# A second layer in seven products on four token-tile pairs, with the low halves on GpSimd

## The chip, the cores and the metric

The kernel runs on one core of one Trainium2 chip. The time is device microseconds of that core, from one launch that does everything; the figure of a kernel is the median of its runs. The profile is one execution, recorded by the hardware profiler.

## The reference

Three stages follow each other: an attention with fixed masks, a mixture of experts whose weights P come from a Sinkhorn balancing, and a second mixture that routes each token to two experts. The change lies in the middle stage:

```python
def _moe_ref(x, w_gate, w1, w2):          # x: 1152 x 512, 8 experts, hidden size 1024
    ...
    for e in range(E):
        h = np.maximum(x @ w1[e], 0.0)    # first layer:  1152 x 512 @ 512 x 1024
        ye = h @ w2[e]                    # second layer: 1152 x 1024 @ 1024 x 512
        out += P[:, e:e + 1] * ye
    return out
```

## The kernel before

Every large product is made in three matmuls. Each operand is split into a high half (fp32r) and a low half, the rest that the rounding left; a product is high by high, high by low and low by high, and the fourth term is dropped. ScalarE (ACT) writes the high halves as a copy or a relu, and another engine subtracts to get the low ones.

The middle stage treats experts 1 to 6 in 24 quarters: six experts, and in each four slices of 256 of the hidden size (`quarters`). Expert 0 comes before them and expert 7 after, both by other code. In a quarter:

- The **first layer** is done in two column units, `v` and `w` (`Unit(0)` and `Unit(1)`), of 256 and 320 token columns in each of two token halves. Each unit forms its 2 x 2 block product in seven block products instead of eight (p1 to p7; 42 matmuls per unit). The price is sums of blocks ahead (of the weights, of the activations `sh`, `sl`) and sums of results behind (steps `b`, `d`, `c` on VectorE, here DVE, which read one PSUM bank and one kept copy `s1` or `s5`).
- The results are hidden blocks. ACT writes their high halves, DVE their low ones out of PSUM. Those of unit `v` (token tiles 0, 1 and 7, 8) stand in `hah`, `hal`; those of unit `w` (tiles 2 to 6) in `hbh`, `hbl`.
- The **second layer** takes tiles 0 and 7 as one pair and 1 and 8 as another (class `Two`), again in seven products, each three matmuls of 256 columns. That needs four sums of hidden blocks (`mix`, on DVE, into `us`), split into `hah[:, 3:]` by ACT and `hal[:, 3:]` by DVE. Tiles 2 to 6 are done one by one (`single`): two slices of the hidden size, three matmuls each, of 512 columns.
- Each finished part is scaled with P and added into `acc` by DVE (`add`, L886; `single`, L926). A pair has five such additions of 256 columns and one of 512, a single tile one of 512.
- The weights of the next quarter are made ready meanwhile. SP fetches two pieces of 512 KB (`fetch1`, `fetch2`), GpSimd (POOL) forms eight weight sums of 128x256 (`sums1` into `raw`, `sums2` into `vt`), ACT writes the high halves `u1h`, `u2h`. The low halves are shared out: DVE makes all four blocks of `u1l` and two of `u2l`, POOL the other two of `u2l`.

PE, DVE, ACT and POOL run their instructions in the order in which the code issues them (`tc.manual_schedule`); each waits on semaphores for what it reads or overwrites. `quarter(n)` is that order, written by hand; it is the same for all quarters but for small exceptions in the first (the last steps of the balancing of P, the rescaling of `acc` by `rescale`) and the last (the weights of expert 7, `a0`).

Of the kernel before, what the change touches and what calls it, by code (L numbers as in the profile page):

```python
# [21 lines left out]
NT = N // 128  # L22
# [41 lines left out]
def tile_kernel(ctx: ExitStack, tc: tile.TileContext, qL, kL, vL, qS, kS, vS, wg, u12, w1, w2, wgn, noise, v1, v2, cst, masks, dummy, out):  # L64
# [596 lines left out]
    tags[:] = ["a", "c"]  # L661
# [63 lines left out]
    pair = pair_cm.__enter__()  # L725
    fa = pair.tile([128, 2, 256], F32, name="fa")
    ha = [pair.tile([128, 7, 256], F32R, name=n) for n in ("hah", "hal")]
    hb = [pair.tile([128, 2, 640], F32R, name=n) for n in ("hbh", "hbl")]
    stock, side = (rpool.tile([128, 4, 512], F32, tag="raw", name="raw") for _ in range(2))
    spare = pair.tile([128, 2, 512], F32, name="spare")  # L730
    raws, raw2 = [x.rearrange("p a (b n) -> p (a b) n", b=2) for x in (stock[:, :2], spare)], stock[:, 2:]
    ut = side[:, :2].rearrange("p a n -> p (a n)")
    vt = pair.tile([128, 4, 256], F32, name="vt")
    us = side[:, 2:].rearrange("p a (b n) -> p (a b) n", b=2)
    quarters = [(e, q) for e in range(1, E - 1) for q in range(NP)]

    def fetch1(n):
        if n < len(quarters):
            nc.sync.dma_start((stock[:, :2], spare)[n % 2], u12[quarters[n]][:, :2])

    def fetch2(n):
        nc.sync.dma_start(raw2, u12[quarters[n]][:, 2:])

    def high(hi, src):
        seen[0] = nc.scalar.activation(hi, src, AF.Copy)  # L745

    def low(hi, lo, src, pool=False):
        (nc.gpsimd if pool else nc.vector).tensor_tensor(lo, src, hi.bitcast(F32), op=ALU.subtract)  # L748

    def sums1(n):  # L750
        raw1 = raws[n % 2]
        b11, b21, b12, b22 = (raw1[:, 2 * k:2 * k + 2, j * 128:(j + 1) * 128] for j in range(2) for k in range(2))
        t = [ut[:, o * 256:(o + 1) * 256].rearrange("p (b n) -> p b n", b=2) for o in range(4)]
        for o, x, y in ((0, b12, b11), (2, b22, b12), (1, b22, t[0]), (3, b21, t[1])):
            nc.gpsimd.tensor_tensor(t[o], x, y, op=ALU.subtract)  # L755

    def sums2():
        b11, b12, b21, b22 = (raw2[:, k, n * 256:(n + 1) * 256] for k in range(2) for n in range(2))
        for o, x, y in ((0, b12, b11), (2, b12, b22), (1, b22, vt[:, 0]), (3, b21, vt[:, 1])):
            nc.gpsimd.tensor_tensor(vt[:, o], x, y, op=ALU.subtract)  # L760

    def flat(x):
        return x.rearrange("p a b n -> p (a b) n")

    def first_weights(n):
        raw1 = raws[n % 2]
        blocks = [(flat(u1h[:, :2]), flat(u1l[:, :2]), raw1[:, :, :128])]
        for o in (0, 2):
            t = ut[:, o * 256:(o + 2) * 256].rearrange("p (c n) -> p c n", n=128)
            blocks.append((flat(u1h[:, 3 + o:5 + o]), flat(u1l[:, 3 + o:5 + o]), t))  # L770
        blocks.append((u1h[:, 2], u1l[:, 2], raw1[:, 2:, 128:]))
        return blocks

    def second_weights():
        hi, lo = (pair.tile([128, 8, 256], F32R, tag=t, name=t, bufs=2) for t in ("u2h", "u2l"))
        b = raw2.rearrange("p k (m n) -> p (k m) n", m=2)
        return (hi, lo), [(hi[:, i:i + 2], lo[:, i:i + 2], b[:, i:i + 2] if i < 4 else vt[:, i - 4:i - 2]) for i in range(0, 8, 2)]

    class Unit:
        def __init__(self, u):  # L780
            self.u, self.w = u, WIDE[u]
            self.bank = {}

        def product(self, k, b, x, first):
            if first:
                self.bank[k] = ps(k, k)
            p = self.bank[k][:, :self.w]
            i = 0
            for c in range(2):
# [5 lines left out]
                for l, m in ((u1h, r[0]), (u1h, r[1]), (u1l, r[0])):  # L795
                    nc.tensor.matmul(p, l[:, b, c], m, start=first and i == 0, stop=i == 5, skip_group_check=not first)
                    i += 1
            return p

        def keep(self, name, p):  # L800
            s = ring.tile([128, WIDE[1]], F32, tag=name, name=name)[:, :self.w]
            nc.scalar.activation(s, p, AF.Copy)
            return s

        def high(self, p, m, j):
            if self.u:
                o = hb[0][:, j, m * 320:(m + 1) * 320]
            else:
                o = ha[0][:, m + j]
                if m == j:  # L810
                    nc.scalar.activation(fa[:, j], p, AF.Relu)
            seen[0] = nc.scalar.activation(o, p, AF.Relu)

        def low(self, p, m, j):
            h, l = (x[:, j, m * 320:(m + 1) * 320] if self.u else x[:, m + j] for x in (hb if self.u else ha))
            nc.vector.scalar_tensor_tensor(l, p, 0.0, h.bitcast(F32), op0=ALU.max, op1=ALU.subtract)

        def done(self, p, m, j):
            self.high(p, m, j)
            self.low(p, m, j)  # L820

        def p1(self):
            self.s1 = self.keep("s1", self.product("a", B11, 0, True))

        def p5(self):
            self.s5 = self.keep("s5", self.product("b", T1, 3, True))

        def p6(self):
            p = self.product("a", T2, 4, False)
            nc.vector.tensor_tensor(self.bank["b"][:, :self.w], p, self.s5, op=ALU.add)  # L830

        def p2(self):
            self.c11 = p = self.product("d", B21, 1, True)
            nc.vector.tensor_tensor(p, p, self.s1, op=ALU.add)
            self.high(p, 0, 0)

        def end2(self):
            self.low(self.c11, 0, 0)

        def p7(self):  # L840
            p = self.product("a", T3, 5, False)
            self.c22 = q = ps("c", "c")[:, :self.w]
            nc.vector.tensor_tensor(q, p, self.s5, op=ALU.add)
            self.high(q, 1, 1)

        def end7(self):
            self.low(self.c22, 1, 1)

        def p3(self):
            self.c12 = self.product("b", B22, 6, False)  # L850
            self.high(self.c12, 0, 1)

        def end3(self):
            self.low(self.c12, 0, 1)

        def p4(self):
            p = self.product("a", T4, 2, False)
            self.c21 = p
            if self.u:
                self.high(p, 1, 0)  # L860

        def mix(self, *which):
            terms = ((3, self.c21, fa[:, 0], ALU.subtract), (0, self.c21, fa[:, 1], ALU.add),
                     (1, self.c22, us[:, 3], ALU.add), (2, self.c12, us[:, 1], ALU.subtract))
            for i in which:
                o, x, y, op = terms[i]
                nc.vector.scalar_tensor_tensor(us[:, o], x, 0.0, y, op0=ALU.max, op1=op)  # L867

        def end4(self):
            self.low(self.c21, 1, 0)  # L870

    sums = [(ha[0][:, i:i + 2], ha[1][:, i:i + 2], us[:, i - 3:i - 1]) for i in (3, 5)]

    class Two:
        def __init__(self, e, u2, t, tt, banks):
            self.e, self.u2, self.t, self.tt, self.banks = e, u2, t, tt, banks

        def product(self, o, a, b, first):
            h, l = (x[:, a, self.t * 128:(self.t + 1) * 128] for x in ha)
            r, s = (x[:, b] for x in self.u2)  # L880
# [591 lines left out]
```

## Time and profile before

| | |
|---|---|
| median of 3 runs | 1088.15 us (1087.52 to 1088.39) |
| profiled execution | 1086.06 us, its span 1084.2 us |
| TensorE (PE) busy | 1066.0 us, 98% |
| VectorE (DVE) busy | 774.9 us, 71% |
| ScalarE (ACT) busy | 454.4 us, 42% |
| GpSimd (POOL) busy | 313.7 us, 29% |
| granted TensorE clock, mean | 0.995 of full speed |

The shares are averages over the whole kernel. The profiled execution took 1.9 us more than its span, and 2.1 us less than the median of the runs.

### The profile page before, as it was taken

The numbers are of one execution on the slowest core, as the hardware profiler recorded it, in microseconds if no ns is written. First come the engines' busy times: TensorE is split into PE (matmuls) and PEld (weight loads), VectorE is DVE, ScalarE is ACT, GpSimd is POOL, SyncE is SP. The second block draws the span as 40 slices with busy tenths as digits, with TensorE's granted clock in tenths as the row PEclk, the third lists the DMA queues.
The fourth block names the chain that finished last, engine by engine and source line by source line (L and its number), as shares of the span: only waits on it lengthen the run. The fifth ranks groups of instructions, "written<-read, shape, count | busy, mean of one in ns | idle before, by whom it ended". The sixth has DMA issues, their size and how long they took to land. (4 is left out here: it accounts for less than half of the span.)

```text
span 1084.2 us, 18865 instructions
## 1 busy us (share of the span) xinstructions
PE 1066.0 (98%) x7272; PEld 964.0 (89%) x7272; DVE 774.9 (71%) x1705; ACT 454.4 (42%) x1063; POOL 313.7 (29%) x346
## 2 busy tenths in 40 slices
PE   8999999999999999999999999999999999999996
PEld 5778998999999999999999999998888898888885
DVE  6964879888888888888888888864265465445440
ACT  6651426445334444334444334431133254444541
POOL 2205025433334334334333334100041532233211
PEclk9999999999999999999999999999999999999998
DMA  9321611111112111111111120132103574666531
GB/s 354 138 79 40 191 40 54 46 40 40 40 49 70 40 40 40 40 59 60 40 40 40 40 73 26 40 117 78 47 14 127 176 269 107 209 208 208 188 101 23
DMA packets 35052, 98.26 MB, mean 91 GB/s; under 512 B 6866, under 2 KB 15570, under 8 KB 29456
## 3 DMA queue, kind: packets, MB, share of 16 engines
q1 hardware_dynamic: 19648, 78.95, 20.1%
q0 software_dynamic: 5408, 11.26, 4.9%
q10 hardware_dynamic: 9904, 6.83, 2.0%
q8 instruction: 58, 0.95, 0.4%
q14 instruction: 34, 0.28, 0.1%
HBM read 85.51 MB, written 11.60 MB: 90 GB/s over the span
## 5 line engine op out<-in xcount | busy, mean ns | idle before, releaser
L886 DVE SCALAR_TENSOR_TENSOR acc<-y,P,acc 128x256 f32<-128x256 f32 (+1 forms) x288 | 135.7, 519 | 0.0
L748 POOL TENSOR_TENSOR u2l<-vt,u2h 128x512 fp32r<-128x512 f32 x48 | 62.2, 1312 | 171.5 <-ACT u2h L745 171.5
L161 PE MATMUL h<-xh,wh 128*128 128x384 f32 (+8 forms) x352 | 109.4, 311 | 0.5 <-DVE hl L110 0.5
L161 PE MATMUL h<-xl,wh 128*128 128x384 f32 (+8 forms) x352 | 109.4, 311 | 0.0
L161 PE MATMUL h<-xh,wl 128*128 128x384 f32 (+8 forms) x352 | 109.0, 310 | 0.0
L882 PE MATMUL y<-u2h,hah 128*128 128x256 f32 x336 | 94.9, 282 | 1.5 <-DVE raw L867 1.1
L882 PE MATMUL y<-u2h,hal 128*128 128x256 f32 x336 | 95.1, 283 | 0.0
L882 PE MATMUL y<-u2l,hah 128*128 128x256 f32 x336 | 95.1, 283 | 0.0
L161 PE MATMUL y<-u2h,hbh 128*128 128x512 f32 x240 | 94.3, 393 | 0.0
L161 PE MATMUL y<-u2l,hbh 128*128 128x512 f32 x240 | 94.2, 393 | 0.0
L161 PE MATMUL y<-u2h,hbl 128*128 128x512 f32 x240 | 93.4, 389 | 0.0
L926 DVE SCALAR_TENSOR_TENSOR acc<-y,P,acc 128x512 f32<-128x512 f32 x120 | 85.3, 743 | 0.6 <-PE y L161 0.6
L109 ACT ACTIVATE hh<-h 128x256 fp32r<-128x256 f32 (+2 forms) x88 | 35.4, 414 | 93.8 <-PE h L161 82.2
L110 DVE SCALAR_TENSOR_TENSOR hl<-h,hh 128x256 fp32r<-128x256 f32 (+2 forms) x88 | 40.2, 463 | 38.6 <-ACT hh L109 38.6
L882 PEld LDWEIGHTS y<-u2h,hah 128*128 128x128 f32 x336 | 64.0, 190 | 4.1 <-issue 1.3
L161 PEld LDWEIGHTS h<-xh,wh 128*128 128x128 f32 x352 | 66.2, 188 | 1.6 <-DVE hl L110 1.2
L161 PEld LDWEIGHTS h<-xl,wh 128*128 128x128 f32 x352 | 66.2, 188 | 0.8 <-issue 0.4
L161 PEld LDWEIGHTS h<-xh,wl 128*128 128x128 f32 x352 | 66.2, 188 | 0.5 <-DVE wl L748 0.3
L755 POOL TENSOR_TENSOR raw<-raw 128x256 f32<-128x256 f32 x48 | 35.5, 751 | 106.1 <-DVE u1l L748 65.1
L882 PEld LDWEIGHTS y<-u2l,hah 128*128 128x128 f32 x336 | 64.0, 190 | 1.8
L882 PEld LDWEIGHTS y<-u2h,hal 128*128 128x128 f32 x336 | 64.3, 191 | 0.0
L114 DVE TENSOR_TENSOR wl<-raw,wh 128x1024 fp32r<-128x1024 f32 x40 | 47.1, 1221 | 22.2 <-ACT wh L112 20.0
(294 smaller groups left out, 3197.7 us busy)
## 6 DMA issues: line engine op xcount, KB each, us to landing
raw<-in_v SPq DMA_DIRECT2D x20, 1024.0 KB, 10.8
raw<-in_u SPq DMA_DIRECT2D x36, 512.0 KB, 5.0
acc<-in_v SPq DMA_DIRECT2D x12, 1024.0 KB, 6.8
raw<-in_u SPq DMA_DIRECT2D x7, 1024.0 KB, 4.8
spare<-in_u SPq DMA_DIRECT2D x12, 512.0 KB
raw<-in_w SPq DMA_DIRECT2D x4, 1024.0 KB, 4.8
out<-zero ACTq DMA_DIRECT2D x1, 3072.0 KB, 18.3
vs<-in_vL SPq DMA_DIRECT2D x4, 576.0 KB, 6.6
```

Of the source, the lines that this page charges most:

```text
L109: seen[0] = nc.scalar.activation(hi, src, AF.Relu)
L110: lows.append(nc.vector.scalar_tensor_tensor(lo, src, 0.0, hi.bitcast(F32), op0=ALU.max, op1=ALU.subtract))
L114: nc.vector.tensor_tensor(lo, src, hi.bitcast(F32), op=ALU.subtract)
L161: nc.tensor.matmul(o, a, b, start=start, stop=stop)
L748: (nc.gpsimd if pool else nc.vector).tensor_tensor(lo, src, hi.bitcast(F32), op=ALU.subtract)
L755: nc.gpsimd.tensor_tensor(t[o], x, y, op=ALU.subtract)
L882: nc.tensor.matmul(o, x, y, start=first and n == 0, stop=n == 2, skip_group_check=not first)
L886: nc.vector.scalar_tensor_tensor(o, p, P[:, t, self.e:self.e + 1], o, op0=ALU.mult, op1=ALU.add)
L926: nc.vector.scalar_tensor_tensor(acc[:, t], p, P[:, t, e:e + 1], acc[:, t], op0=ALU.mult, op1=ALU.add)
```

## The change

**Second layer.** Tiles 2 and 5 become a pair, and 3 and 6 another; tile 4 alone stays single (class `One`). `operands` finds a pair's blocks: for tiles 0 and 1 in `ha` as before, for tiles 2 and 3 in `hb` and, for the sums of blocks, in the new tiles `hs`. Unit `w` now makes the four sums too (`m0` to `m3`, `f0`, `f1`, `S0`, `S1`, `L0`, `L1`). Of its block c21 only the first 64 columns, those of tile 4, are still split.

**Engines.** In the quarters, every low half that is a difference of two SBUF operands, of weights and of sums, is made by GpSimd. DVE keeps the low halves out of PSUM, the sums of results and the additions into `acc`. There are exceptions ahead of the first quarter and in it (the first `u1l`, and `Y0`, `Y1`, the first blocks of `u2l`), which stay on DVE.

**Order.** The work of a quarter is cut into small steps with names, and three lists give their order for all engines: `FIRST` for the first quarter, `STEPS` for 22, and `FINAL` for the last. A step with "-" belongs to the quarter before: the second halves of the pairs run into the next quarter. `spare`, `u2` and the fetches are doubled so that weights can be fetched two quarters ahead. In expert 0 the two PSUM tags of the second layer change places.

```diff
-    with tc.manual_schedule(...): for n in range(len(quarters)): quarter(n)
+    sums = [[(*(x[:, o + i:o + i + 2] for x in y), us[:, i:i + 2]) for i in (0, 2)] for o, y in ((3, ha), (0, hs))]
+    def low(block, engine=nc.vector):
+        engine.tensor_tensor(block[1], block[2], block[0].bitcast(F32), op=ALU.subtract)
+    def operands(a, t):
+        if t < 2:
+            return [x[:, a, t * 128:(t + 1) * 128] for x in ha]
+        o = t * 128 - 256
+        if a > 2:
+            return [x[:, a - 3, o:o + 128] for x in hs]
+        o += 384 * (a == 2)
+        return [x[:, int(a > 0), o:o + 128] for x in hb]
...
+            if kind in "qz":
+                nc.gpsimd.tensor_tensor(o, x, y, op=ALU.subtract)
+            elif half == "h":
+                high(getattr(self, kind)[i])
+            else:
+                low(getattr(self, kind)[i], nc.gpsimd)
...
+            self.A, self.B = Two(e, w, 0, 7, "ab"), Two(e, w, 1, 8, "dc")
+            self.C, self.D = Two(e, w, 2, 5, "dc"), Two(e, w, 3, 6, "ab")
...
+    STEPS = """
+        -D.p6 -D.p5 -C.p6 -D.e6 -w.L1 -C.p5 v.p1 -D.p7 -D.e5 -D.p3 y0h -C.e6 z0 -B.p4 -s4.e -x2h -C.e5 -B.e4
...
+        v.m3 y2l v.h2 w.p2 v.l1 y3l v.m1 v.S0 w.b A.p2 q3 v.l2 v.m2 -C.e3 v.L0 w.d w.p7 y1h v.S1 w.c A.p1 w.h0
```

In the lists, `x`, `y` are blocks of the weights of the first and second layer with `h` and `l` for their halves, `q`, `z` the weight sums, `p` products on PE, `e` additions into `acc`, `f1`, `f2` fetches.

**What GpSimd executes in a quarter.** Before, a whole quarter is these five rows (`raw`, `vt`: weight sums; `u2l`: low halves of second-layer weights):

```order
L755 TENSOR_TENSOR raw<-spare 128x256 x2
L755 TENSOR_TENSOR raw<-spare,raw 128x256 x2
L760 TENSOR_TENSOR vt<-raw 128x256 x2
L760 TENSOR_TENSOR vt<-raw,vt 128x256 x2
L748 TENSOR_TENSOR u2l<-vt,u2h 128x512 x2
```

Now a quarter of the steady kind begins with one row for `vt` and one for `raw`, and goes on with these twelve (L882 is `low`, L988 the weight sums):

```order
L882 TENSOR_TENSOR u1l<-spare_1906,u1h 128x256
L882 TENSOR_TENSOR u2l_1915<-raw,u2h_1914 128x512
L882 TENSOR_TENSOR u1l<-raw,u1h 128x512
L988 TENSOR_TENSOR vt<-raw,vt 128x256 x2
L988 TENSOR_TENSOR vt<-raw 128x256
L988 TENSOR_TENSOR raw<-raw 128x256 x2
L882 TENSOR_TENSOR u2l_1915<-vt,u2h_1914 128x512 x2
L988 TENSOR_TENSOR raw<-raw 128x256
L882 TENSOR_TENSOR hal<-raw,hah 128x512 x2
L882 TENSOR_TENSOR u2l_1915<-raw,u2h_1914 128x512
L882 TENSOR_TENSOR u1l<-raw,u1h 128x512 x2
L882 TENSOR_TENSOR hsl<-raw,hsh 128x512 x2
```

GpSimd had ten instructions in a quarter, eight of 256 columns and two of 512; it has twenty, nine of 256 and eleven of 512. They stand between each other in one queue.

**What VectorE executes about the middle of a quarter.** `b<-a,s` of 320 columns is step `w.b`: it must be done before PE may overwrite bank `a` with the product p7 of unit `w`. Before:

```order
L816 SCALAR_TENSOR_TENSOR hal<-c,hah 128x256
L816 SCALAR_TENSOR_TENSOR hal<-b,hah 128x256
L867 SCALAR_TENSOR_TENSOR raw<-a,fa 128x256 x2
L830 TENSOR_TENSOR b<-a,s_3847 128x320
L867 SCALAR_TENSOR_TENSOR raw<-c,raw 128x256
L867 SCALAR_TENSOR_TENSOR raw<-b,raw 128x256
L834 TENSOR_TENSOR d<-d,s_3819 128x320
L886 SCALAR_TENSOR_TENSOR acc<-y,P,acc 128x256
L816 SCALAR_TENSOR_TENSOR hbl<-d,hbh 128x320
L843 TENSOR_TENSOR c<-a,s_3847 128x320
L748 TENSOR_TENSOR hal<-raw,hah 128x512
```

Now (L850 is a sum of hidden blocks, L823 a low half out of PSUM, L906 an addition into `acc`):

```order
L823 SCALAR_TENSOR_TENSOR hal<-d,hah 128x256
L850 SCALAR_TENSOR_TENSOR raw<-a,fa 128x256 x2
L823 SCALAR_TENSOR_TENSOR hal<-b,hah 128x256
L850 SCALAR_TENSOR_TENSOR raw<-c,raw 128x256
L794 TENSOR_TENSOR b<-a,s_4106 128x320
L823 SCALAR_TENSOR_TENSOR hal<-c,hah 128x256
L850 SCALAR_TENSOR_TENSOR raw<-b,raw 128x256
L906 SCALAR_TENSOR_TENSOR acc<-y,P,acc 128x256
L797 TENSOR_TENSOR d<-d,s_4088 128x320
L801 TENSOR_TENSOR c<-a,s_4106 128x320
L823 SCALAR_TENSOR_TENSOR hbl<-d,hbh 128x320
```

The low half of a sum (L748) is gone from DVE, an addition of the quarter before has moved in, and one more sum stands ahead of `b`. On PE there are fewer matmuls at this place: before, PE issued w.p6, w.p2, then the products p2 and p1 of the first pair (six matmuls), then w.p7; now it issues w.p6, w.p2, only p2 of the first pair (three matmuls), then w.p7.

## Rows read from the trace of the kernel before

**Rows 1.** Page, busy us of each engine (share of the span), instructions

```profile
PE 1066.0 (98%) x7272; PEld 964.0 (89%) x7272; DVE 774.9 (71%) x1705; ACT 454.4 (42%) x1063; POOL 313.7 (29%) x346
```

**Rows 2.** By stretch: length, busy us of PE, PEld, DVE, ACT, POOL; clock, DMA

```profile
158.60:182.00 23.40, 21.89 (x152) 20.42 (x151) 21.89 (x47) 17.46 (x36) 15.44 (x16) 1.00 0.14 46
182.00:704.00 522.00, 522.00 (x3531) 494.24 (x3530) 454.29 (x950) 222.08 (x519) 184.05 (x223) 1.00 0.14 46
```

**Rows 3.** Timeline of PE in a steady quarter: start us, us, instruction, count

```profile
505.06 0.28 PE L796 MATMUL a<-xh,u1h 128*128 128x256 f32 x1
...
506.50 0.40 PE L161 MATMUL y<-u2h,hbh 128*128 128x512 f32 x1
...
509.25 0.28 PE L796 MATMUL a<-sh,u1h 128*128 128x256 f32 x1
...
513.00 0.31 PE L796 MATMUL b<-sh,u1h 128*128 128x320 f32 x1
...
513.88 0.28 PE L796 MATMUL a<-xh,u1h 128*128 128x256 f32 x1
...
515.34 0.31 PE L796 MATMUL a<-sh,u1l 128*128 128x320 f32 x1
...
517.08 0.31 PE L796 MATMUL a<-sh,u1h 128*128 128x320 f32 x1
...
528.16 0.28 PE L796 MATMUL a<-xh,u1h 128*128 128x256 f32 x1
```

**Rows 4.** Who waited for whom, PE, in the first quarter: us, times, longest

```profile
PE y L882 <- DVE raw L867: 1.1, 1, 1.1
PE y L882 <- DVE acc L886: 0.4, 1, 0.4
```

**Rows 5.** Timeline of DVE in the quarter of rows 3; [idle before <- releaser]

```profile
514.80 0.75 DVE L867 SCALAR_TENSOR_TENSOR raw<-a,fa 128x256 f32<-128x256 f32 x2 [0.41 <-PE a L796]
515.75 0.50 DVE L830 TENSOR_TENSOR b<-a,s 128x320 f32<-128x320 f32 x1 [0.20 <-PE a L796]
...
522.12 2.19 DVE L886 SCALAR_TENSOR_TENSOR acc<-y,P,acc 128x256 f32<-128x256 f32 x4
524.22 1.40 DVE L926 SCALAR_TENSOR_TENSOR acc<-y,P,acc 128x512 f32<-128x512 f32 x2
525.54 0.68 DVE L748 TENSOR_TENSOR u1l<-raw,u1h 128x512 fp32r<-128x512 f32 x1
526.14 1.65 DVE L886 SCALAR_TENSOR_TENSOR acc<-y,P,acc 128x256 f32<-128x256 f32 x4
527.71 0.68 DVE L748 TENSOR_TENSOR u1l<-raw,u1h 128x512 fp32r<-128x512 f32 x1
```

**Rows 6.** Timeline of POOL, the first quarter (first line) and that of rows 3

```profile
164.27 3.01 POOL L748 TENSOR_TENSOR u2l<-vt,u2h 128x512 fp32r<-128x512 f32 x2
...
511.72 1.44 POOL L760 TENSOR_TENSOR vt<-raw 128x256 f32<-128x256 f32 x2 [0.45 <-DMA raw<-in_u]
513.11 1.56 POOL L760 TENSOR_TENSOR vt<-raw,vt 128x256 f32<-128x256 f32 x2
522.71 2.56 POOL L748 TENSOR_TENSOR u2l<-vt,u2h 128x512 fp32r<-128x512 f32 x2 [8.05 <-ACT u2h L745]
```

**Rows 7.** Line 748: duration ns min/median/max, first and last start, shape

```profile
L748 POOL TENSOR_TENSOR u2l<-vt,u2h x48: 1287/1296/1748, 164.3 to 685.7; 128x512 fp32r<-128x512 f32 x48
L748 DVE TENSOR_TENSOR u2l<-raw,u2h x48: 674/679/1787, 165.4 to 692.0; 128x512 fp32r<-128x512 f32 x48
```

**Rows 8.** Timeline of the first quarter, PE (first line) and DVE

```profile
158.86 0.28 PE L796 MATMUL a<-xh,u1h 128*128 128x256 f32 x1
...
159.67 0.22 DVE L393 TENSOR_REDUCE rs<-P 128x9 f32<-128x72 f32 x1
...
161.35 0.29 DVE L398 TENSOR_REDUCE c<-P 128x8 f32<-128x72 f32 x1
...
165.45 2.39 DVE L748 TENSOR_TENSOR u2l<-raw,u2h 128x512 fp32r<-128x512 f32 x2
```

More of the change, by code (lines that the diff above doesn't have):

```diff
@@ L734, in tile_kernel @@
     us = side[:, 2:].rearrange("p a (b n) -> p (a b) n", b=2)
[L735 to L777, printed above, removed]
@@ L781, in __init__, with product @@
             self.u, self.w = u, WIDE[u]
-            self.bank = {}
-        def product(self, k, b, x, first):
+            self.bank, self.kept = {}, {}
+        def product(self, k, b, x):
+            first = k not in self.bank
             if first:
-                self.bank[k] = ps(k, k)
-            p = self.bank[k][:, :self.w]
+                self.bank[k] = ps(k, k)[:, :self.w]
             i = 0
@@ L795, in product @@
                 for l, m in ((u1h, r[0]), (u1h, r[1]), (u1l, r[0])):
-                    nc.tensor.matmul(p, l[:, b, c], m, start=first and i == 0, stop=i == 5, skip_group_check=not first)
+                    nc.tensor.matmul(self.bank[k], l[:, b, c], m, start=first and i == 0, stop=i == 5, skip_group_check=not first)
                     i += 1
[L798 to L815, printed above, removed]
-            nc.vector.scalar_tensor_tensor(l, p, 0.0, h.bitcast(F32), op0=ALU.max, op1=ALU.subtract)
@@ L818, in done @@
[L818 to L867, printed above, removed]
@@ L869, in end4, with p1, p5, p6 @@
-        def end4(self):
-            self.low(self.c21, 1, 0)
-    sums = [(ha[0][:, i:i + 2], ha[1][:, i:i + 2], us[:, i - 3:i - 1]) for i in (3, 5)]
+        def p1(self):
+            self.product("a", B11, 0)
+        def p5(self):
+            self.product("b", T1, 3)
+        def p6(self):
+            self.product("a", T2, 4)
+        def p2(self):
+            self.product("d", B21, 1)
+        def p7(self):
+            self.product("a", T3, 5)
+        def p3(self):
+            self.product("b", B22, 6)
@@ new lines, in p4, with keep, k1, k5 @@
+        def p4(self):
+            self.product("a", T4, 2)
+        def keep(self, name, k):
+            self.kept[name] = ring.tile([128, WIDE[1]], F32, tag=name, name=name)[:, :self.w]
+            nc.scalar.activation(self.kept[name], self.bank[k], AF.Copy)
+        def k1(self):
+            self.keep("s1", "a")
+        def k5(self):
+            self.keep("s5", "b")
+        def b(self):
+            nc.vector.tensor_tensor(self.bank["b"], self.bank["a"], self.kept["s5"], op=ALU.add)
+        def d(self):
+            nc.vector.tensor_tensor(self.bank["d"], self.bank["d"], self.kept["s1"], op=ALU.add)
@@ new lines, in c, with mine, f0, f1 @@
+        def c(self):
+            self.bank["c"] = ps("c", "c")[:, :self.w]
+            nc.vector.tensor_tensor(self.bank["c"], self.bank["a"], self.kept["s5"], op=ALU.add)
+        def mine(self, k, m):
+            x = self.bank[k]
+            return x[:, m * 64:m * 64 + 256] if self.u else x
+        def f0(self):
+            nc.scalar.activation(fa[:, 0], self.mine("d", 0), AF.Relu)
+        def f1(self):
+            nc.scalar.activation(fa[:, 1], self.mine("c", 1), AF.Relu)
+        def values(self, k, m, j):
+            p = self.bank[k][:, :64] if self.u and k == "a" else self.bank[k]
+            return p, [x[:, j, m * 320:m * 320 + p.shape[1]] if self.u else x[:, m + j] for x in (hb if self.u else ha)]
@@ new lines, in m1, with m2, S0, S1 @@
+        def m1(self):
+            self.mix(1, "c", 1, us[:, 3], ALU.add)
+        def m2(self):
+            self.mix(2, "b", 0, us[:, 1], ALU.subtract)
+        def S0(self):
+            high(sums[self.u][0])
+        def S1(self):
+            high(sums[self.u][1])
+        def L0(self):
+            low(sums[self.u][0], nc.gpsimd)
+        def L1(self):
+            low(sums[self.u][1], nc.gpsimd)
+    sums = [[(*(x[:, o + i:o + i + 2] for x in y), us[:, i:i + 2]) for i in (0, 2)] for o, y in ((3, ha), (0, hs))]
@@ L928, in rescale, with e1 @@
-    def rescale(n, *tiles):
-        if n == 0:
-            for t in tiles:
-                nc.scalar.activation(acc[:, t], acc[:, t], AF.Copy, scale=P[:, t, :1])
-    def run(*steps):
-        for s in steps:
-            s()
-    def highs(*blocks):
-        for hi, lo, src in blocks:
-            high(hi, src)
-    def lows_of(*blocks, pool=False):
-        for hi, lo, src in blocks:
-            low(hi, lo, src, pool)
+        def e1(self):
+            self.add(self.c, self.t, slice(0, 256))
@@ L945, in tile_kernel, with fetch1, fetch2, rescale @@
+    quarters = [(e, q) for e in range(1, E - 1) for q in range(NP)]
+    LAST = len(quarters) - 1
+    def fetch1(n):
+        if n <= LAST:
+            nc.sync.dma_start((stock[:, :2], spare[0])[n % 2], u12[quarters[n]][:, :2])
+    def fetch2(n):
+        if n <= LAST:
+            nc.sync.dma_start(raws[n % 2][1], u12[quarters[n]][:, 2:])
+    def rescale(*tiles):
+        for t in tiles:
+            nc.scalar.activation(acc[:, t], acc[:, t], AF.Copy, scale=P[:, t, :1])
     fetch1(0)
     fetch2(0)
-    sums1(0)
@@ L1034, in tile_kernel @@
-    with tc.manual_schedule(engines={mybir.EngineType.PE, mybir.EngineType.DVE, mybir.EngineType.Activation, mybir.EngineType.Pool}):
-        for n in range(len(quarters)):
-            quarter(n)
-        run(*rest)
-        lows_of(*x[2:])
+    fetch1(1)
+    fetch2(1)
+    parts = [Weights(0)]
+    for k, i in (("q", 0), ("q", 2), ("q", 1), ("q", 3), ("z", 0), ("z", 2), ("z", 1), ("z", 3)):
+        parts[0].step(k, i, "")
+    for i in range(4):
+        high(parts[0].x[i])
+        low(parts[0].x[i])
@@ new lines, in tile_kernel, with perform @@
+    ONCE.update({f"Y{i}": partial(low, parts[0].y[i]) for i in range(2)})
+    work = {}
+    wpool = None
+    def perform(n, name):
+        late = name[0] == "-"
+        name = name.lstrip("-")
+        m = n - late
+        if name in ("f1", "f2"):
+            if 0 <= m:
+                (fetch1 if name == "f1" else fetch2)(m + 2)
+        elif "." not in name:
+            if 0 <= m < LAST:
+                if m + 1 >= len(parts):
+                    parts.append(Weights(m + 1))
+                parts[m + 1].step(name[0], int(name[1]), name[2:])
+        elif 0 <= m <= LAST:
+            if m not in work:
+                work[m] = Quarter(m)
+            who, what = name.split(".")
+            who = getattr(work[m], who)
+            (who.add if name == "s4.e" else getattr(who, what))()
@@ new lines, in tile_kernel @@
+    with tc.manual_schedule(engines={mybir.EngineType.PE, mybir.EngineType.DVE, mybir.EngineType.Activation, mybir.EngineType.Pool}):
+        balance_rows()
+        column_sums("d")
+        balance_columns()
+        for n in range(LAST + 1):
+            for name in FIRST if n == 0 else FINAL if n == LAST else STEPS:
+                if wpool is None and name == "a0h":
+                    wpool = enter()
+                if name in ONCE:
+                    ONCE[name]()
+                else:
+                    perform(n, name)
```

247 lines of the change are left out of this document (136 added, 111 removed).

## The prediction, written before the changed kernel was run

> **What bounds the kernel now.** I read the page first: PE is busy for 1066.0 us, 98% of the span, every other engine for less than three quarters of the span [rows 1]. An average hides the stages, so next I cut the span by stage. In the 22 steady quarters, a stretch of 522 us, PE is busy for all 522.00 us at the full clock, while DVE has 454.29, ACT 222.08 and POOL 184.05 [rows 2]. So in this stage nothing that DVE, ACT or POOL does can shorten the time; only fewer or shorter matmuls can. The reader should see the other side of this too: DVE, at 87%, has the least room, and POOL, at 35%, the most.
>
> Busy spans overlap on a pipelined engine, so for costs I took the timeline and the distance from one start to the next. On PE [rows 3]: twelve matmuls of 256 columns from 505.06 to 506.50 are 0.120 us each, twelve of 512 from 506.50 to 509.25 are 0.229, six of 320 from 513.00 to 513.88 are 0.147. A quarter lasts from 505.06 to 528.16, which is 23.10 us. Check: 42 x 0.120 and 42 x 0.147 for the first layer, 42 x 0.120 for two pairs, 30 x 0.229 for five single tiles: 5.04 + 6.17 + 5.04 + 6.87 = 23.12. The quarter is its matmuls and nothing else.
>
> Last I looked at where PE does stand still in this part: in the first quarter, 1.5 us in two waits, both on DVE [rows 4].
>
> **The change, step by step.**
>
> *PE.* Two single tiles cost 12 x 0.229 = 2.75 us; a pair costs 21 x 0.120 = 2.52. The pair saves 0.23 us although it has nine matmuls more, since 21 x 256 columns are fewer than 12 x 512. Two new pairs in each of 24 quarters: 48 x 0.23 = 11.0 us. The quarter becomes 5.04 + 6.17 + 10.08 + 1.37 = 22.66 us, if PE never waits. This is the one term that is a gain by itself; everything below asks whether the other engines keep up with 22.66.
>
> *DVE.* Steps from [rows 5]: an addition of 256 columns 0.39 (526.14 to 527.71, four), of 512 0.66 (524.22 to 525.54, two), a low half of 512 columns 0.60 (525.54 to 526.14), a sum of hidden blocks at most 0.38 (two in 0.75). Removed per quarter: three low halves of u1l, two of u2l and two of hal, 7 x 0.60, a short one of u1l, half of that, and four single additions, 4 x 0.66: 7.1 us. Added: two pairs with 5 x 0.39 + 0.66 each and four sums, 5.2 + 1.5 = 6.7 us. DVE had 454.29 / 522 x 23.10 = 20.1 us in a quarter [rows 2] and will have about 19.7 of 22.66. It stays hidden.
>
> *POOL.* It takes over nine instructions of 512 columns and one of 256. Steps from [rows 6]: 1.27 us for 512 (two in 2.56, one 1.29 long), 0.70 for 256 (from 511.72 to 513.11, two), at most 0.86 where an instruction needs the result of the one before (1.56 - 0.70). A quarter has eleven of 512, five independent ones of 256 and four dependent ones: 11 x 1.27 + 5 x 0.70 + 4 x 0.86 = 20.9 us, against 184.05 / 522 x 23.10 = 8.1 before. So POOL goes from 35% to 92% of the quarter and has 1.8 us left, under 0.1 us for each of its 20 instructions. What covers this work is the same PE time; without the cover the excess over 22.66 would appear whole.
>
> Would DVE and POOL hold each other up? Subtractions by POOL took 1296 ns in the median and up to 1748, the same kind on DVE 679 and up to 1787 [rows 7]. The long ones lie in the first quarter, where the two engines subtract SBUF operands at the same time: two in 3.01 on POOL from 164.27, two in 2.39 on DVE from 165.45 [rows 6, 8]. Beside DVE's additions and sums, which read PSUM and one SBUF operand, POOL kept to 1.29 (at 522.71, with DVE on additions from 522.12 on [rows 5, 6]). In the steady quarters no DVE instruction with two SBUF operands is left, so I cost the contention at nothing there. The Trainium skill, "SBUF — State Buffer", section "SBUF: two separate sides", says that GpSimd and a VectorE instruction with two SBUF inputs exclude each other for a whole instruction. By that rule, too, the sum would not change, because the change takes such instructions off DVE; the trace agrees in the 1787.
>
> *ACT.* Four instructions more, two high halves of sums and two relu copies, on 222.08 / 522 x 23.10 = 9.8 us a quarter. Its 519 instructions take 0.43 us in the mean; at twice that, 13.2 of 22.66 [rows 2]. It costs nothing beside PE.
>
> *Fetches.* As many as before, issued two quarters ahead into doubled buffers. POOL's wait of 0.45 for one [rows 6] should go; it was no cost.
>
> *A wait that comes nearer.* PE may not write w.p7 into bank a before DVE has read it in w.b. Before: last matmul of w.p6 at 515.34, w.b from 515.75 to 516.25, w.p7 at 517.08 [rows 3, 5], a margin of 0.83 us. Now three matmuls stand between instead of six: w.p7 is due 3 x 0.120 earlier, so the margin is 0.47, and DVE has one sum more to do ahead of w.b. Behind a late w.p7 stands the whole of PE. I take no wait; both ends are in the rivals.
>
> *First quarter.* PE lost 1.5 us there [rows 4]. Now the matmul of the column sums stands behind 24 matmuls, at 158.86 + 2.88 = 161.7. On DVE the row balancing, 2.0 us from 159.67 to 161.64 [rows 8], gets a low half Y1 ahead of it (0.60, or up to 1.79 if POOL holds it [rows 7]): ready at 162.2 to 163.4. PE waits 0.5 to 1.7. In exchange the first waits may vanish, since the low halves for which DVE was late are mostly on POOL. I take 1.5 again, so no change, with 0 to 3 as bounds: 1.5 us either way.
>
> *Last quarter.* POOL makes the low weights for expert 7 at its end, four of 512 columns, 5.1 us, beside tail products of two pairs. I take nothing, bounded by one such instruction, 1.3 us.
>
> *Sum.* 1086.06 - 11.0 = 1075.1 us for the profiled execution; the runs' median stood 2.1 above that one, so **1088.15 - 11.0 = 1077.2 us**, a gain of 1.0%. A difference within 0.2%, some 2.2 us, could not be told from no change.
>
> **Rivals.**
>
> *Small waits in each quarter.* DVE or POOL is late by some tenths each time, at w.p7 (margin 0.47) or where PE needs `hsl` just behind the quarter's start. DVE's whole free time is 3 us in a quarter, and additions of the old quarter now stand in its queue among the steps of the new one. For it: the one late sum held PE for 1.1 us in the first quarter [rows 4]. Against: w.b started 0.41 us after its operand's last matmul, waiting for PE itself [rows 5]. If DVE is 0.3 us later than the margin allows, 22 x 0.3 = 6.6 us are given back: 1083.8. At 0.46 the gain is gone.
>
> *POOL becomes the bound: slower than before.* Its place is the queue of twenty, its price 22 quarters times what they exceed 22.66. It decides at a known point: 23.10 - 20.9 = 2.2 us, or 0.11 us more per instruction, and the kernel is as slow as before. If each took the 0.45 us more of the longest in [rows 7], a quarter would need 29.9 us and the kernel 1088 + 22 x 6.8 = 1238 us. For it: 92% load, in order, with waits on ACT for high halves ahead of most instructions. Against: 1287 to 1296 from the minimum to the median.
>
> *A matmul hardly gets cheaper with fewer columns.* Then 21 would cost more than 12. If one of 256 cost the 0.147 of 320 columns, a pair would take 3.09 us and the change lose 48 x 0.34 = 16 us: 1104. The rows exclude it for just this product: 0.120 over long series. The Trainium skill, "TensorE: Matmul & The Clock Gate", section "Back-to-back issue gap", gives sustained spacings of 81 ns for 128 columns and 131 ns for 512. An estimate from these, 98 ns for 256, would make a pair 2.05 us against 1.57 and the kernel 48 x 0.48 = 23 us slower; the trace, with 229 ns for 512, does not bear it out here.
>
> **How the numbers follow.** Forecast as it stands, PE without waits: 0.78, 1074.6 to 1080. Small waits: 0.12, 1080 to 1086. POOL the bound: 0.09, of which half ends near the old time and half slower. Cheap columns: 0.01. The low end is 11.0 plus the 1.5 of the first quarter plus 0.9, the spread of the runs: 1074.7. The high end is the rival with 0.3 us per quarter, 1083.8. Together: faster 0.91, same 0.04, slower 0.05.
>
> **What would show it.** Right: PE busy through all steady quarters, a quarter of 22.6 to 22.7 us from one product p1 of unit v to the next; POOL about 20 us in each, its subtractions still near 1.29 and 0.74; DVE about 19.7. Wrong: PE waits for DVE at w.p7 or for POOL at `hsl`, in every quarter; instructions on POOL above 1.4 us; PE losing more than 3 us in the first quarter.

## The result and the profile after

| | before | after |
|---|---|---|
| median | 1087.84 us (4 runs, 1087.43 to 1088.39) | 1077.63 us (4 runs, 1075.06 to 1079.24) |
| profiled execution | 1086.06 us, span 1084.2 | 1077.3 us, span 1075.1 |
| granted clock, mean | 0.995 | 0.997 |

The ratio is 0.9904, with a 95% interval of 0.9883 to 0.9924: faster by 10.2 us. The forecast was 1077.2 us.

The page's line of busy times, which answers to [rows 1]:

```profile
PE 1056.0 (98%) x7704; PEld 976.6 (91%) x7704; DVE 754.5 (70%) x1803; ACT 497.0 (46%) x1159; POOL 597.9 (56%) x584
```

PE has 432 matmuls more and is busy for 10 us less. POOL's busy time has nearly doubled, and the share of PE is still 98%: the bound is where it was.

By stretch (length, busy us of PE, PEld, DVE, ACT, POOL, granted clock, DMA), the first quarter and the steady ones, as in [rows 2]:

```profile
159.20:182.00 22.80, 22.12 (x166) 21.34 (x165) 20.38 (x50) 17.08 (x38) 20.53 (x21) 1.00 0.16 49
182.00:690.00 508.00, 508.00 (x3903) 502.23 (x3903) 431.54 (x1032) 260.03 (x603) 446.71 (x441) 1.00 0.15 46
```

PE is busy for 508.00 of 508.00 us. POOL's 446.71 are 19.9 us in a quarter of 22.66, DVE's 431.54 are 19.2, ACT's 260.03 are 11.6.

The timeline of PE over one steady quarter (start us, us, instruction), as in [rows 3]; the first and the last line are product p1 of unit `v` in two quarters that follow each other:

```profile
407.75 0.28 PE L759 MATMUL a<-xh,u1h 128*128 128x256 f32 x1
...
408.47 0.28 PE L902 MATMUL y<-u2h,hsh 128*128 128x256 f32 x1
...
430.41 0.28 PE L759 MATMUL a<-xh,u1h 128*128 128x256 f32 x1
```

From 407.75 to 430.41 is 22.66 us, where [rows 3] had 23.10. Behind the six matmuls of p1 stand products on `hsh` and `hsl`, the halves of sums of the quarter before: the place where a late POOL would hold PE.

POOL in that quarter; in brackets the idle time ahead of an instruction and what ended it:

```profile
408.19 1.32 POOL L882 TENSOR_TENSOR u2l<-raw,u2h 128x512 fp32r<-128x512 f32 x1
409.45 1.33 POOL L882 TENSOR_TENSOR u1l<-raw,u1h 128x512 fp32r<-128x512 f32 x1
410.70 1.59 POOL L988 TENSOR_TENSOR vt<-raw,vt 128x256 f32<-128x256 f32 x2
...
416.76 1.30 POOL L882 TENSOR_TENSOR u2l<-vt,u2h 128x512 fp32r<-128x512 f32 x1 [1.11 <-ACT u2h L879]
...
419.24 2.55 POOL L882 TENSOR_TENSOR hal<-raw,hah 128x512 fp32r<-128x512 f32 x2 [0.49 <-ACT hah L879]
...
426.28 2.56 POOL L882 TENSOR_TENSOR hsl<-raw,hsh 128x512 fp32r<-128x512 f32 x2 [0.71 <-ACT hsh L879]
```

Subtractions of 512 columns keep to 1.30, as at 522.71 in [rows 6], and what POOL waits for is ACT's high halves: 2.3 us in this quarter.

Who waited for whom on PE, from the first quarter to the last (us, times, longest), against [rows 4]:

```profile
PE a L759 <- DVE c L801: 0.5, 1, 0.5
PE cs L403 <- DVE c L399: 0.2, 1, 0.2
```

Both lie in the first quarter, 0.7 us in all where before had 1.5; in the steady quarters there is no row. The wait for `c` has its cause in DVE's queue. The instruction ahead of that step scales P, from two SBUF operands, beside a subtraction on POOL:

```profile
164.68 1.28 DVE L410 TENSOR_TENSOR P<-P,c 128x72 f32<-128x72 f32 x1
```
```profile
164.58 1.30 POOL L882 TENSOR_TENSOR u2l<-spare,u2h 128x512 fp32r<-128x512 f32 x1
```

It ends 0.08 us after POOL's instruction and took 1.28 us, where the same one took 0.69 in the kernel before; step `c` stands right behind it. Experiment 3 shows this holding up in every quarter.

One of the 22 steady quarters, from 316.94, took 22.83 us and not 22.66. A pause of PE too short for a row of its own is the reason (see the last section).

**The account by stage.** From the first p1 to the first matmul of expert 7 the stage took 556.85 us before and takes 545.76 now, 11.1 less. The window from that point to the end, first of the kernel before:

```profile
715.71:1084.20 368.49, 355.93 (x2226) 313.68 (x2224) 174.69 (x396) 140.84 (x249) 83.08 (x65) 0.99 0.42 135
```

And of the changed kernel:

```profile
705.06:1075.10 370.04, 356.33 (x2225) 313.83 (x2225) 174.83 (x398) 140.75 (x249) 82.86 (x65) 0.99 0.43 134
```

This later part is 1.55 us longer, and expert 0 ahead of the stage 0.44 longer (p1 at 159.30, not 158.86): 11.1 - 1.55 - 0.44 = 9.1 us, the difference of the two spans. The medians of the runs differ by 10.2, since the profiled execution of before was 1.8 us below its median and that of after 0.3 below. In the profiles of the eight experiments p1 came between 158.6 and 160.1, so 0.44 is within what single executions differ by.

### The profile page after: what moved, and what is told of

It reads as the page before. It is cut to its first block, busy times and chain, and to the rows that moved or that the text cites. A ratio compares the mean times of both kernels' runs of the same rounds, so it can differ in the third digit from the quotient of the medians.

```text
span 1075.1 us, 20369 instructions
## 1 busy us (share of the span) xinstructions
PE 1056.0 (98%) x7704; PEld 976.6 (91%) x7704; DVE 754.5 (70%) x1803; ACT 497.0 (46%) x1159; POOL 597.9 (56%) x584
## 4 chain that ended last, share of the span: by engine, by line
PE 91%; DVE 5%; ACT 1%; issue 1%; DMA 0%; POOL 0%; POOLq 0%; DVEq 0%; ACTq 0%
PE y L902 22%; PE y L161 20%; PE h L161 18%; PE a L759 14%; PE b L759 7%; PE d L759 3%; PE y L1217 2%; PE xgt L1125 1%; DVE wl L114 1%; DVE acc L906 1%; PE sc L231 1%; PE sc L220 1%; DVE u1l L114 1%; DMA raw<-in_v 0%; ACT spread L246 0%
## 5 line engine op out<-in xcount | busy, mean ns | idle before, releaser
L906 DVE SCALAR_TENSOR_TENSOR acc<-y,P,acc 128x256 f32<-128x256 f32 (+1 forms) x576 | 275.1, 522 | 9.6 <-PE y L902 5.0
L1203 POOL DMA_INDIRECT out<-y,tt x23 | 38.4, 1668 | 83.1 <-ACT y L1221 43.6
L882 POOL TENSOR_TENSOR u2l<-vt,u2h 128x512 fp32r<-128x512 f32 x48 | 62.3, 1300 | 36.1 <-ACT u2h L879 36.1
L882 POOL TENSOR_TENSOR u1l<-raw,u1h 128x512 fp32r<-128x512 f32 (+1 forms) x68 | 81.9, 1212 | 0.0
L558 POOL DMA_INDIRECT table<-en,si x18 | 18.5, 1030 | 106.0 <-DVE parts L476 76.8
L623 POOL DMA_INDIRECT xg<-x2d,tt x23 | 23.5, 1023 | 91.2 <-PE xgt L1125 71.6
L882 POOL TENSOR_TENSOR hal<-raw,hah 128x512 fp32r<-128x512 f32 x48 | 61.2, 1298 | 23.3 <-ACT hah L879 23.3
L882 POOL TENSOR_TENSOR hsl<-raw,hsh 128x512 fp32r<-128x512 f32 x48 | 61.5, 1300 | 15.6 <-ACT hsh L879 15.6
```

The lines of the kernel that those rows point to most:

```text
L558: st = nc.gpsimd.indirect_dma_start(out=table[:, :], out_offset=bass.IndirectOffsetOnAxis(ap=si[:, i, k:k + 1], axis=0), in_=en[:, i, k], ...
L623: nc.gpsimd.indirect_dma_start(out=xg[:n], out_offset=None, in_=x2d[:rows, :], in_offset=bass.IndirectOffsetOnAxis(ap=tt[:n, 0:1], axis=0))
L882: engine.tensor_tensor(block[1], block[2], block[0].bitcast(F32), op=ALU.subtract)
L906: nc.vector.scalar_tensor_tensor(o, p, P[:, t, self.e:self.e + 1], o, op0=ALU.mult, op1=ALU.add)
L1203: st = nc.gpsimd.indirect_dma_start(out=out[:, :], out_offset=bass.IndirectOffsetOnAxis(ap=tt[:k, 0:1], axis=0), in_=y[:k], in_offset=None ...
```

## The experiments

All eight start from the changed kernel; their times are medians, with the ratio to the kernel before, which ran again beside them (1087.49 us beside experiments 1 to 4, 1087.77 beside 5 to 8).

**1. The new pairs as single tiles again** (`singles`). Tiles 2, 3, 5 and 6 are done one by one, with the block c21 split whole; the order, the engines and the sums of unit `w` stay, and nothing reads those sums.

```diff
-            self.C, self.D = Two(e, w, 2, 5, "dc"), Two(e, w, 3, 6, "ab")
+            self.C, self.D = Singles(e, w, 2, 5, "dc"), Singles(e, w, 3, 6, "ab")
```

> Tiles 2, 3, 5 and 6 are done one by one again, with 12 matmuls of 512 columns for two tiles in place of 21 of 256. Everything else of the change stays: low halves on GpSimd, the three lists, and even the sums of unit w, whose results nobody reads now; its block c21 is split over all 320 columns again. Theory (the gain is TensorE's columns, all else is hidden): a quarter goes from 22.66 back to 23.1 us, the kernel to 1077.6 + 48 x 0.23 = 1088.6 us, within 2. Rival (the gain comes from taking subtractions off VectorE and from the new order): within 3 us of 1077.6.

Measured: 1087.9 us (1087.04 to 1088.94), ratio 1.0004 [0.9995, 1.0014]. By stretch:

```profile
182.00:700.00 518.00, 518.00 (x3498) 489.28 (x3497) 378.09 (x850) 258.63 (x602) 448.36 (x442) 1.00 0.13 45
```

PE is busy for all 518.00 us, and the quarter is 23.12 us (like matmuls of line 759 at 391.30 and 414.42). So the shift of work to POOL and the new order give nothing by themselves; the whole gain is the products of the two pairs. That the shift and the order are needed to keep this gain is what experiments 3, 4 and 8 show.

**2. w.b two steps later** (`wb_late`). On DVE, step `w.b` moves behind a low half and a sum; PE's order stays.

```diff
-        v.m3 y2l v.h2 w.p2 v.l1 y3l v.m1 v.S0 w.b A.p2 q3 v.l2 v.m2 -C.e3
+        v.m3 y2l v.h2 w.p2 v.l1 y3l v.m1 v.S0 A.p2 q3 v.l2 v.m2 w.b -C.e3
```

> In the steady list, step w.b is issued behind v.l2 and v.m2 on VectorE, 0.34 + 0.38 = 0.72 us later. Theory (the margin of 0.47 us ahead of w.p7 is what the rows of before gave): TensorE waits 0.25 us in each of 22 quarters, 5.5 us, 1083 us. Rival 1 (VectorE has caught up by then, the margin is larger): 1077.6, within 2. Rival 2 (w.b was late already and the margin near nothing): up to 0.72 x 22 = 15.8 us, 1093.

Measured: 1088.63 us (1087.46 to 1089.56), ratio 1.0007 [0.9997, 1.0017]: the whole gain is gone. The timeline of DVE in the changed kernel at this place:

```profile
259.29 0.42 DVE L850 SCALAR_TENSOR_TENSOR raw<-c,raw 128x256 f32<-128x256 f32 x1 [0.49 <-ACT hah L819]
259.63 0.49 DVE L794 TENSOR_TENSOR b<-a,s 128x320 f32<-128x320 f32 x1
```

PE there, the last matmul of w.p6 and the first of w.p7:

```profile
259.02 0.31 PE L759 MATMUL a<-sh,u1l 128*128 128x320 f32 x1
...
260.40 0.31 PE L759 MATMUL a<-sh,u1h 128*128 128x320 f32 x1
```

The same of DVE in this experiment, a quarter of its own:

```profile
401.01 0.49 DVE L794 TENSOR_TENSOR b<-a,s 128x320 f32<-128x320 f32 x1
```

And of PE, from the last matmul of w.p6 to the second of w.p7:

```profile
399.74 0.31 PE L759 MATMUL a<-sh,u1l 128*128 128x320 f32 x1
...
401.00 0.28 PE L902 MATMUL y<-u2h,hal 128*128 128x256 f32 x1
401.56 0.41 PE L759 MATMUL a<-sh,u1h 128*128 128x320 f32 x1 [0.28 <-DVE b L794]
401.81 0.30 PE L759 MATMUL a<-sl,u1h 128*128 128x320 f32 x1
```

In the changed kernel w.b ends at 260.12 and w.p7 starts at 260.40. Its margin is 0.28 us, and the handover takes 0.06 of it, as w.p7 here starts that much after w.b's end at 401.50. The prediction had 0.47. The reason stands in the row ahead of w.b: a sum of hidden blocks that waits 0.49 us for a high half from ACT, so that w.b starts 0.61 us after the last matmul of w.p6, where it was 0.41 [rows 3, 5]. In the experiment it starts 1.27 after. The quarter shown is the usual one: the margin is 0.28 in 21 of the 22 steady quarters and 0.06 in the one of 22.83 us.

The second reading is what a wait costs PE. The wait's row says 0.28 us. But from the last matmul ahead of it to w.p7 is 0.56 us, where 0.12 is the step: 0.44 lost. The records of matmuls are longer than the steps between them, and so hide 0.16 of a pause. The next step is 0.25 instead of 0.147: another 0.10. Together 0.54 us, which is what the quarter grew by (23.20 - 22.66); 22 x 0.54 = 11.9 us, and 11.0 were measured.

**3. The low halves of the sums on DVE** (`sums_dve`). `hal` and `hsl` of the sums leave POOL; everything else stays.

```diff
-            low(sums[self.u][0], nc.gpsimd)
+            low(sums[self.u][0])
-            low(sums[self.u][1], nc.gpsimd)
+            low(sums[self.u][1])
```

> The low halves of the four sums of hidden blocks go back to VectorE (hal and hsl), those of the weights stay on GpSimd. By load alone VectorE has 19.7 + 4 x 0.60 = 22.1 us in a quarter of 22.66 and GpSimd 20.9 - 4 x 1.27 = 15.8. Theory (the two engines exclude each other when both subtract SBUF operands): each of the four waits for a running GpSimd instruction, 0.3 to 0.8 us, VectorE needs 23.3 to 25.3 us, the kernel 1092 to 1136. Rival (only the load counts): all still hidden, below 1081.

Measured: 1156.11 us (1155.96 to 1156.25), ratio 1.0629 [1.0608, 1.0650]. DVE first, then POOL:

```profile
405.10 1.74 DVE L882 TENSOR_TENSOR hal<-raw,hah 128x512 fp32r<-128x512 f32 x1
...
408.43 0.68 DVE L882 TENSOR_TENSOR hal<-raw,hah 128x512 fp32r<-128x512 f32 x1
...
415.47 1.75 DVE L882 TENSOR_TENSOR hsl<-raw,hsh 128x512 fp32r<-128x512 f32 x1
```
```profile
405.00 1.29 POOL L882 TENSOR_TENSOR u2l<-raw,u2h 128x512 fp32r<-128x512 f32 x1 [1.00 <-ACT u2h L879]
...
415.39 1.29 POOL L882 TENSOR_TENSOR u2l<-spare,u2h 128x512 fp32r<-128x512 f32 x1 [0.51 <-ACT u2h L879]
416.64 1.74 POOL L882 TENSOR_TENSOR u1l<-raw,u1h 128x512 fp32r<-128x512 f32 x1
```

The same subtraction takes DVE 0.68 us when POOL rests (408.43, POOL idle until 409.25) and 1.74 when POOL has begun one 0.10 earlier; it ends 0.55 after POOL's end at 406.29. At 415.47 the same again. At 416.64 it is POOL's turn: it starts while DVE subtracts, and takes 1.74 instead of 1.29. So the two take turns, a whole instruction at a time. That is what the Trainium skill says under "SBUF — State Buffer", section "SBUF: two separate sides", of a GpSimd instruction that reads SBUF and a VectorE instruction with two SBUF inputs, and these rows agree. PE's waits from 182 to 690 us:

```profile
PE a L759 <- DVE c L801: 19.1, 19, 1.1
PE y L902 <- DVE hsl L882: 16.4, 20, 1.0
```

The long subtraction at 405.10 delays the steps `d` and `c` behind it in DVE's queue, and the next product waits for `c`. A quarter takes 26.15 us, though DVE (179.84 us in a stretch of 200) is not full: order and lock, not load. The theory was right about the lock, but 1156 is above its upper end of 1136. It took DVE's load for the bound. DVE's busy time did come as expected, 23.5 us in a quarter, but PE waits for single late operands, and DVE stands idle for 2.6 us of the quarter itself.

**4. Four pairs with the low halves shared as before** (`share_before`). DVE makes them all but two of the second layer's weights.

```diff
-                low(getattr(self, kind)[i], nc.gpsimd)
+                low(getattr(self, kind)[i], nc.gpsimd if kind == "y" and i > 1 else nc.vector)
```

With the edit of experiment 3 as well.

> The second layer in four pairs, but the low halves shared out as before: on VectorE all of u1l, two blocks of u2l and the sums, on GpSimd two blocks of u2l. Theory (without the move to GpSimd, VectorE cannot carry the two new pairs): its load is 19.7 + 9 x 0.60 + 0.3 = 25.4 us in a quarter, 2.7 more than TensorE's 22.66, so at least 1077.6 + 22 x 2.7 = 1137 us, and with waits for GpSimd's instructions up to 1190. Rival (the move was not needed, TensorE stays the bound): below 1090.

Measured: 1200.68 us (1200.59 to 1200.76), ratio 1.1039 [1.1017, 1.1061]; a quarter of 28.0 us. PE's waits, whole span:

```profile
PE a L759 <- DVE u1l L882: 32.7, 22, 1.5
PE y L161 <- DVE hbl L823: 11.1, 22, 0.5
PE y L902 <- DVE acc L906: 8.9, 25, 0.4
PE y L902 <- DVE hsl L882: 7.8, 21, 0.4
```

These are the four longest, and all are on DVE. It is busy for 177.96 us in a stretch of 200, which is 24.9 us in a quarter, more than PE's 22.66; 25.4 were expected. The measured time is 11 us above the expected upper end, since DVE waits for 3.1 us of the quarter as well. In this order, then, the two halves of the change belong together: the seven products without the shift to POOL cost 113 us instead of saving 10. The order, though, was written for the low halves on POOL; what the best order for this share would give wasn't tried.

**5 to 7. POOL with two, four and six more additions of 256 columns in a quarter** (`pool_2`, `pool_4`, `pool_6`). Weight sums are formed twice; DVE, ACT and PE keep their work. The edit of the second, the third also doubles `z1` and `q1`, the first only `z0` and `q0`:

```diff
-... y0h -C.e6 z0 -B.p4 ...  v.p6 q0 v.p5 ...  -D.p4 z2 -D.e4 ...  v.c q2 -D.e3 ...
+... y0h -C.e6 z0 z0 -B.p4 ...  v.p6 q0 q0 v.p5 ...  -D.p4 z2 z2 -D.e4 ...  v.c q2 q2 -D.e3 ...
```

> In the steady list two weight sums of 128x256 (z0 and q0) are computed twice on GpSimd, 0.70 to 0.86 us each, with the same results. Theory (GpSimd needs 20.9 us of 22.66 and has some 1.8 left): 22.4 us, still hidden, 1077.6 us within 2. Rival (GpSimd is at its limit already, so that each addition shows): 22 x 1.5 = 33 us more, 1110.

> Four weight sums (z0, q0, z2, q2) are computed twice on GpSimd in each steady quarter. Theory by the sum of the prediction (20.9 + 4 x 0.75 = 23.9 us against 22.66): 22 x 1.2 = 27 us more, 1105. By the busy time in the trace of the changed kernel (446.71 us in 508, 19.9 a quarter, + 2.8 to 3.4): 22.7 to 23.3, 1079 to 1092. Rival (GpSimd is far from binding): 1077.6.

> Six weight sums (z0, q0, z2, q2, z1, q1) are computed twice on GpSimd in each steady quarter. Theory (GpSimd's queue is the bound from some point on): the two further instructions show whole, 22 x 1.4 to 1.7 = 31 to 38 us more than with four. Rival (a single late operand sets the time, not the load of the queue): within 10 us of the kernel with four.

| | median us | ratio | quarter us | POOL busy of 200 us |
|---|---|---|---|---|
| after, none | 1077.63 (1075.06 to 1079.24) | 0.9904 [0.9883, 0.9924] | 22.66 | 178.41 |
| two | 1077.82 (1077.37 to 1078.28) | 0.9907 [0.9891, 0.9924] | 22.66 | 191.64 |
| four | 1096.07 (1095.33 to 1096.80) | 1.0076 [1.0056, 1.0096] | 23.49 | 196.55 |
| six | 1130.52 (1129.37 to 1131.67) | 1.0393 [1.0372, 1.0414] | 25.07 | 195.60 |

PE in a quarter of the last, around its two long waits:

```profile
397.32 0.28 PE L902 MATMUL y<-u2l,hah 128*128 128x256 f32 x1
398.45 0.39 PE L902 MATMUL y<-u2h,hal 128*128 128x256 f32 x1 [0.85 <-POOL hal L882]
398.67 0.28 PE L902 MATMUL y<-u2h,hah 128*128 128x256 f32 x1
...
400.54 0.39 PE L902 MATMUL y<-u2h,hah 128*128 128x256 f32 x1 [0.65 <-DVE acc L906]
```

The second wait comes from POOL too. The addition that PE waits for stands in DVE's queue behind a sum that had to wait for POOL's `hal`:

```profile
399.67 0.43 DVE L850 SCALAR_TENSOR_TENSOR raw<-a,fa 128x256 f32<-128x256 f32 x1 [2.44 <-POOL hal L882]
```

Two are free. From four to six each addition costs (25.07 - 23.49) / 2 = 0.79 us of the quarter, between the 0.70 and 0.86 that an addition takes on POOL in [rows 6]: POOL is the bound there. Counted back, the changed kernel's POOL needs 23.49 - 4 x 0.79 = 20.3 us. Two additions make 21.9, still below 22.66, as the second row of the table bears out. By this working the reserve is 2.4 us, three such additions (three were not run); the prediction had 20.9 and 1.8. With four, 1096 us lie between the two expectations, 1105 by the prediction's 20.9 and at most 1092 by the busy time, which leaves out the pauses of 0.08 us that POOL makes ahead of a sum that needs the one before it. As the bound, POOL reads 98% busy, not 100.

**8. The plain order in the first and last quarter too** (`plain_ends`). The lists `FIRST` and `FINAL` are replaced by `STEPS` with the steps that only these quarters have put in, and without those that they lack.

```diff
-        z0 z2 Y1 y0h v.p1 br v.k1 Y0 v.p5 v.p2 v.p6 z1 v.k5 z3 y2h cs v.d v.b ...
+        -D.p6 -D.p5 -C.p6 -D.e6 -w.L1 -C.p5 v.p1 Y1 br Y0 -D.p7 -D.e5 -D.p3 y0h -C.e6 z0 -B.p4 ...
```

> The first and the last quarter take the steady list: in the first the balancing, the rescaling and the two low halves Y0, Y1 are put in, in the last the weights of expert 7 stand in the second half, and the late steps of the last quarter follow at its end. Theory (all of the gain comes from the 22 steady quarters and from the pairs, the own lists of the ends only avoid waits): 1077.6 us and up to 3 us more for each end, 1077.6 to 1083.6; the trace shows at which end. Rival (the own lists are worth nothing): 1077.6 within 2. Rival (they carry the gain): 1087 or more.

Measured: 1084.36 us (1082.50 to 1084.70), ratio 0.9962 [0.9948, 0.9976]. PE's waits from 150 to 740 us:

```profile
PE y L902 <- POOL hsl L882: 2.0, 1, 2.0
PE h L161 <- DVE acc L906: 1.4, 1, 1.4
PE a L759 <- ACT s L785: 0.9, 1, 0.9
PE a L759 <- DVE b L794: 0.7, 1, 0.7
...
```

The steady quarters are as they were (22.65). The first grows from 21.68 to 23.82 us, and the last waits 2.0 us for `hsl`, whose POOL work stands behind the weights of expert 7; 1.4 more fall at the start of expert 7. The separate order at the two ends is worth 6.7 us of the 10.2, a little more than the upper bound expected.

## Why the prediction was right

**PE.** The mechanism is shown: experiment 1 takes the products away, and the gain goes with them, and the quarter is 22.66 to the hundredth. The size agrees less well than the totals say. The stage got 11.1 us shorter, but 0.8 of it are the shorter waits of the first quarter, so the 48 pairs gave some 10.3 where 11.0 were forecast. A quarter gained 0.44 and not 0.46, since it had been 23.10 before and the sum made it 23.12. That the two differences nearly cancel is luck.

**DVE.** Predicted 19.7 us in a quarter, measured 19.2. The sum left out that of block c21 only 64 columns are still split: 0.21 us for that low half, where 320 columns took 0.49. The share didn't need to be exact, since PE hardly waited for it in the steady quarters.

**POOL.** Predicted 20.9 us, found 20.3 by experiments 5 to 7. The term was 0.6 too high. Four additions were costed as dependent at 0.86, but only one in a quarter stands right behind the one that it reads (0.85 from its predecessor's start, at 410.70); the others take 0.70, three times 0.16 less. The eleven of 512 columns take 1.25 to 1.26 and not 1.27, which is the rest. The rival "POOL the bound" didn't come, but it is a real one, at the place that the prediction gave it: four short additions more, and the kernel is slower than before.

**Contention.** Costed at nothing in the steady quarters, as no DVE instruction with two SBUF operands is left there. POOL's subtractions took 1.30 us in the mean there, none above 1.33, and experiment 3 shows what those instructions would have cost. In the first quarter the contention is real: it is behind the wait of 0.5 us at `c`.

**The wait that comes nearer.** The conclusion (no wait) was right for 21 of 22 quarters, and in the other 0.17 us were lost; the size was not right: the margin is 0.28 us, not 0.47. The step that failed is "the margin is 0.47, and DVE has one sum more to do ahead of w.b": that sum was named and not priced, and it waits for ACT and makes w.b start 0.20 later. Also, the rival's price of 0.3 us per quarter for 0.3 us of lateness is too low, since a wait costs PE 0.1 us more at the restart.

**First quarter.** Taken as 1.5 us of waiting either way, measured 0.7: 0.2 at the column sums (0.5 to 1.7 were predicted) and 0.5 further on, at step `c`, where none was predicted. The row balancing finished at 162.49, within the predicted time. Inside the bounds, and 0.8 us better.

**Last quarter.** Nothing was taken, and nothing is there; experiment 8 shows a wait of 2.0 for `hsl` at that very place when the order isn't adapted, more than the 1.3 that the prediction had as the bound.

**What no term covered.** The later part is 1.55 us longer in the profiled executions, though its matmuls are the same in the same order. PE's waits there, before the change:

```profile
PE y L161 <- DVE hl L110: 1.6, 1, 1.6
PE xgt L1055 <- DMA xg<-x2d,tt: 0.7, 1, 0.7
PE h L161 <- DVE hl L110: 0.5, 2, 0.3
```

And after it:

```profile
PE h L161 <- DVE hl L110: 2.7, 3, 2.1
PE h L161 <- issue: 0.7, 1, 0.7
PE ht L1176 <- DVE hl L114: 0.4, 1, 0.4
PE y L161 <- issue: 0.2, 1, 0.2
```

They are 2.8 us before and 4.0 after. Experiment 1, which has the old products in the quarters, has the same long wait (`hl`, 1.8 us at its longest) and the same kind of "issue" wait (0.9), so the pairs are not the cause. Experiments 2 to 7, with the same code from there on, took 369.3 to 371.0 us for this part, all more than the 368.49 of before. Single executions differ by as much as the 1.55, so its size is uncertain, and its cause stays open.

## What to carry to other kernels

When one engine is busy for every microsecond of a stage, cut its work and pay with engines that have room, but move both halves at once: here, in an order made for both, the shorter products alone cost 113 us, and the shift alone gave nothing. Before such a shift count the reserve of the engine that takes over in its own instructions (here three short additions), and keep operations that lock each other out off the two engines in the same stretch. A margin at a buffer that is overwritten is read from the time at which the last operand of the work ahead of it arrives, not from a sum of durations.

## What the runs showed of the hardware

In these traces a wait of PE costs more than its row says. In `wb_late` 0.28 us are shown and 0.54 lost. In `pool_6` 0.85 are shown at 398.45; the step there is 1.13 us and the next 0.22, where 0.12 each is usual, so 1.11 are lost. About 0.16 are hidden under the record of the matmul ahead, and the step behind the restart is 0.10 longer. Short waits come dear, and a pause of PE below 0.16 us behind a matmul of 256 columns has no row at all. The changed kernel has one, in the quarter of 22.83 us:

```profile
328.26 0.28 PE L902 MATMUL y<-u2h,hal 128*128 128x256 f32 x1
328.45 0.42 PE L759 MATMUL a<-sh,u1h 128*128 128x320 f32 x1
```

This is w.p7. Its step is 0.19 us instead of 0.12 and the next 0.25 instead of 0.147, together the 0.17 that the quarter is longer; w.b ended 0.06 ahead of it, because ACT was 0.3 us later than usual with the high half that the sum ahead of w.b waits for. `pool_4`, where a quarter grew by 0.83 us, has one row in it; PE there:

```profile
410.62 0.39 PE L902 MATMUL y<-u2h,hah 128*128 128x256 f32 x1 [0.27 <-DVE acc L906]
```
